# One tile for the high and low part of a weight, and twelve weight slots that begin at twelve places modulo 512 bytes

## The chip, the cores and the metric

The kernel runs on one core of one Trainium2 chip. The metric is the device time of one execution in microseconds. Before the change two runs took 986.48 and 988.05 us; their median is 987.26 us.

## The reference

The kernel computes an attention with a feature map and then two MLPs, all in float32:

```python
proj = einsum('bhsd,df->bhsf', x, w_phi)            # q and k: 4 batches, 8 heads, 576 rows, 64 wide; 128 features
proj = proj - max(abs(proj), axis=-1)
phi  = concatenate([exp(proj), exp(-proj)])
kv   = einsum('bhsf,bhsd->bhfd', phi(k), v); z = sum(phi(k), axis=2)
x    = einsum('bhsf,bhfd->bhsd', phi(q), kv) / (einsum('bhsf,bhf->bhs', phi(q), z) + 1e-06)
x    = x.transpose(0, 2, 1, 3).reshape(2304, 512)
h    = x @ w_in1;  x   = (h * cos(h)) @ w_out1                               # 512 -> 2048 -> 512
h    = x @ w_in2;  out = (max(h, 0) + alpha * min(h, 0)) @ w_out2            # 512 -> 2048 -> 512
```

The four weight matrices arrive as float64, seen by the kernel as pairs of 32-bit words.

## The kernel before

**The products.** A float32 product of the MLPs is made of three float32r matmuls: a number is split into a high part (float32r) and a low part (what is left, again float32r), and `mm3` (L160 to L166) sums high x high, high x low and low x high. Each matmul instruction loads its own stationary operand of 128 columns and then streams a moving operand of 512 or 256 columns past it. In the trace a matmul is named out<-moving,stationary.

**The order.** A step is one layer, one block of 128 of the 2048 hidden features (`ft`) and one group of 512 tokens (the last group has 256): 2 layers x 16 x 5 = 160 steps. `hidden` (L168) makes the hidden features of a step with 12 matmuls: stationary a 128 x 128 piece of the weight `wi` (high or low), moving the tokens `xh` or `xl`. `output` (L217) multiplies them into the output: in layer 0 the weight `wo` is stationary and the gated features `gh`, `gl` move; in layer 1 `gh`, `gl` are stationary and `wo` moves. `moe_step` runs the hidden part of one step, then the output part of an earlier step, and so on: 12 matmuls of `ph`, then 12 of `po` (6 where a layer-1 group has 256 tokens), through both layers.

**The weights.** `fetch_w` loads a 128 x 512 block of a weight as pairs of words. `w_instructions` (L95) lists the ten instructions that turn it into a high and a low part: ScalarE writes the high part (`to_hi`, L111, its copy at L116), GpSimd subtracts it (L134) and writes the low part (L135). These run some steps ahead of the use, at steps that a table `decode_at` holds. There are six slots for `wi` and six for `wo`, used in turn (slot = block number modulo 6). `w_tile` (L90) gives a slot's part a tile of 2048 bytes per partition, high and low apart, each with its own name: `wih0`, `wil0`, `wih1` and so on. Slots 0 and 1 lie in one pool, slots 2 to 5 in a second one, opened when the attention's tiles are closed.

**Where the tiles lie.** In the built program `xh`, `xl`, all 24 weight tiles, all `gh` and `gl` and the accumulators `acc` start 352 bytes past a multiple of 512, and the slices that a matmul takes of them are multiples of 512 bytes apart. So stationary and moving operand of every matmul of the MLPs start at the same place modulo 512. In what follows a tile's *place* is its start modulo 512, counted from the start of `xh`: here it is 0 for all.

**The attention.** It runs first, and its numerator (`num`, L574 to L586) is the one other float32r product: stationary `kvh` or `kvl` of 66 columns, moving `qp0h`, `qp0l` (256 columns) or `qp1h`, `qp1l` (320). A head's 66 columns are 264 bytes, a pair of heads 528, so these stationary operands start at many places, all multiples of 8 bytes and none 0 against their moving operand. The projections (`project`, L456) are plain float32 products. The last two blocks of `num` lie between the first `hidden` parts.

Of the kernel before, what the change touches and what calls it, by code (L numbers as in the profile page):

```python
# [12 lines left out]
F32R = mybir.dt.float32r  # L13
# [8 lines left out]
P = 128  # L22
# [6 lines left out]
def feature_map_attention_two_mlps(  # L29
# [15 lines left out]
    DM, DFF = w_in1.shape  # L45
# [6 lines left out]
    NFT = DFF // P  # L52
# [29 lines left out]
    w_t = {}  # L82
    w_pools, w_temps = [wpool], [wtmp]
    staged, decoding = [], []

    def split(hi, lo, src, lo_engine):
        nc.scalar.copy(hi, src)  # L87
        lo_engine.tensor_tensor(out=lo, in0=src, in1=hi.bitcast(F32), op=ALU.subtract)  # L88

    def w_tile(slot, nm):  # L90
        s = slot % WSLOTS
        pool = w_pools[0 if s < WSLOTS_A else 1]
        return pool.tile([P, DM], F32R, tag=f"{nm}{s}", name=f"{nm}{s}")

    def w_instructions(spare=True):  # L95

        layer, which, ft, st = staged.pop(0)
        w_temps.append(w_temps.pop(0))  # L100
        u = w_temps[0].tile([P, DM], F32, tag="wu", name="wu")
        t = w_temps[0].tile([P, DM], I32, tag="wt", name="wt")
        e = w_temps[0].tile([P, DM], I32, tag="we", name="we")
        w0, w1 = st[:, :, 0], st[:, :, 1]
        tf, ef = t.bitcast(F32), e.bitcast(F32)
        ts, stt = nc.vector.tensor_scalar, nc.vector.scalar_tensor_tensor
        tt = nc.gpsimd.tensor_tensor
        tv, copy = (nc.vector.tensor_tensor, nc.vector.tensor_copy) if spare else (tt, nc.scalar.copy)
        hl = []

        def to_hi():  # L111
            hl.extend(w_tile(layer * NFT + ft, f"w{'io'[which]}{x}") for x in "hl")
            w_t[layer, which, ft] = tuple(
                z.rearrange("p (k f) -> p k f", k=KD) if which == 0 else z for z in hl
            )
            copy(hl[0], tf)  # L116

        return [
            lambda: nc.scalar.activation(out=u, in_=w1.bitcast(F32), func=AF.Abs),
            lambda: ts(  # L120
                out=e, in0=w1, scalar1=0x07FFFFFF, scalar2=3, op0=ALU.bitwise_and,
                op1=ALU.logical_shift_left,
            ),
            lambda: stt(  # L124
                out=t, in0=w1, scalar=-0x40000000, in1=e, op0=ALU.bitwise_and, op1=ALU.bitwise_or
            ),
            lambda: stt(out=tf, in0=u, scalar=MIN_PATTERN, in1=tf, op0=ALU.is_ge, op1=ALU.mult),  # L127
            lambda: ts(out=e, in0=t, scalar1=-0x00800000, scalar2=None, op0=ALU.bitwise_and),
            to_hi,
            lambda: nc.scalar.activation(  # L130
                out=u, in_=w0.bitcast(U32), func=AF.Copy, scale=2.0 ** -52
            ),
            lambda: tt(out=u, in0=u, in1=ef, op=ALU.mult),  # L133
            lambda: tv(out=tf, in0=tf, in1=hl[0].bitcast(F32), op=ALU.subtract),  # L134
            lambda: tv(out=hl[1], in0=tf, in1=u, op=ALU.add),  # L135
        ]
# [140 lines left out]
    for i in range(2 * NFT):  # L277
        for which in range(2):
            w = (i // NFT, which, i % NFT)
# [17 lines left out]
    for latest in late[::-1][2 * WSLOTS_A:2 * W_EVEN]:  # L297
        need, free, w = todo.pop(0)
# [8 lines left out]
    for t in times:  # L307
        ready = [w for w in todo if w[1] <= t]
        if ready and (t > at + 1 or t >= latest[ready[0][2]]):
            need, _, w = ready[0]  # L310
# [490 lines left out]
```

## Time and profile before

| | us |
|---|---|
| median of two runs | 987.26 |
| the profiled execution | 987.01 |
| its span, first to last instruction | 985.2 |
| TensorE busy (matmul) | 978.3 |
| VectorE busy | 687.4 |
| GpSimd busy | 606.5 |
| ScalarE busy | 493.8 |

The profiled execution's own time is 1.8 us above its span. The profile models where a matmul ends: matmuls overlap in the records, so a matmul's duration (some 0.39 us) is longer than the distance from one start to the next, and it is that distance that adds up to the time.

### The profile page before, as it was taken

How to read it: one execution, taken by the hardware profiler on the slowest of the kernel's cores; microseconds unless marked ns; L12 is line 12 of the kernel's file. 1: busy time of each engine (PE TensorE's matmuls, PEld its weight loads, DVE VectorE, ACT ScalarE, POOL GpSimd, SP SyncE). 2: the span in 40 equal slices, each digit the busy share in tenths (PEclk: the TensorE clock that was granted, in tenths of full speed). 3: DMA queues.
4: the chain of work that ended last, by engine and by line, in shares of the span. 5: the costliest groups of instructions: out<-in, count | busy, mean ns of one | idle time of the engine just before them, and what ended most of it. 6: DMA issues, size and time to landing. Idle time of an engine off the chain costs nothing.

```text
span 985.2 us, 13990 instructions
## 1 busy us (share of the span) xinstructions
PE 978.3 (99%) x5141; PEld 839.2 (85%) x5141; DVE 687.4 (70%) x977; ACT 493.8 (50%) x967; POOL 606.5 (62%) x498
## 2 busy tenths in 40 slices
PE   9999999999999999999999999999999999999998
PEld 7999999888888888888888888888888888888886
DVE  6868686677987577747774788588748874885343
ACT  5888788867666467546755654132213221322110
POOL 3577777856666467535756789567636763676221
PEclk9999999999999999999999999999999999999999
DMA  7454543211111112101210112012101210110112
GB/s 165 113 140 124 142 121 109 70 48 56 52 66 45 42 43 65 44 22 43 65 44 22 44 43 65 22 43 65 43 22 44 65 43 22 43 65 1 43 55 95
DMA packets 64580, 60.63 MB, mean 62 GB/s; under 512 B 28928, under 2 KB 54656, under 8 KB 64512
## 3 DMA queue, kind: packets, MB, share of 16 engines
q1 hardware_dynamic: 64352, 59.68, 20.7%
q8 instruction: 40, 0.66, 0.3%
q14 instruction: 28, 0.23, 0.1%
q10 hardware_dynamic: 160, 0.07, 0.0%
HBM read 52.50 MB, written 4.79 MB: 58 GB/s over the span
## 4 chain that ended last, share of the span: by engine, by line
PE 95%; ACT 1%; DVE 1%; DMA 1%; POOL 1%; issue 0%; ACTq 0%; SPq 0%; DVEq 0%; POOLq 0%
PE po L165 39%; PE ph L165 38%; PE pj L456 6%; PE kv L497 5%; PE nm L581 5%; PE tp L537 1%; DMA dn<-acc 0%; DMA acc<-dr 0%; DMA w<-in_w_phi_dram 0%; DVE acc L616 0%; ACT acc L556 0%; DVE r L192 0%; DVE wt L127 0%; DMA dr<-dn 0%; ACT r L184 0%
## 5 line engine op out<-in xcount | busy, mean ns | idle before, releaser
L88 POOL TENSOR_TENSOR gl<-r,gh 128x512 fp32r<-128x512 f32 (+1 forms) x160 | 204.3, 1278 | 294.0 <-ACT gh L87 289.0
L87 ACT CAST gh<-r 128x512 fp32r<-128x512 f32 (+1 forms) x160 | 92.1, 576 | 381.4 <-DVE r L211 260.9
L165 PE MATMUL ph<-xl,wih 128*128 128x512 f32 (+1 forms) x640 | 236.0, 369 | 0.1
L165 PE MATMUL ph<-xh,wih 128*128 128x512 f32 (+1 forms) x640 | 235.7, 368 | 0.0
L165 PE MATMUL ph<-xh,wil 128*128 128x512 f32 (+1 forms) x640 | 235.6, 368 | 0.0
L245 DVE TENSOR_TENSOR acc<-po,acc 128x512 f32<-128x512 f32 (+1 forms) x134 | 86.1, 659 | 96.5 <-PE po L165 96.5
L165 PEld LDWEIGHTS ph<-xl,wih 128*128 128x128 f32 x640 | 120.7, 189 | 20.7 <-POOL xl L625 0.3
L165 PEld LDWEIGHTS ph<-xh,wih 128*128 128x128 f32 x640 | 120.7, 189 | 20.6
L165 PEld LDWEIGHTS ph<-xh,wil 128*128 128x128 f32 x640 | 120.6, 188 | 20.0
L165 PE MATMUL po<-gh,wol 128*128 128x512 f32 (+1 forms) x320 | 118.0, 369 | 0.2 <-POOL wol L135 0.2
L165 PE MATMUL po<-gl,woh 128*128 128x512 f32 (+1 forms) x320 | 118.0, 369 | 0.0
L165 PE MATMUL po<-gh,woh 128*128 128x512 f32 (+1 forms) x320 | 118.0, 369 | 0.0
L165 PE MATMUL po<-woh,gh 128*128 128x512 f32 x288 | 112.4, 390 | 0.0
L165 PE MATMUL po<-wol,gh 128*128 128x512 f32 x288 | 112.4, 390 | 0.0
L165 PE MATMUL po<-woh,gl 128*128 128x512 f32 x288 | 112.3, 390 | 0.0
L124 DVE SCALAR_TENSOR_TENSOR wt<-ws,we 128x512 int32<-128x512 int32 x64 | 98.4, 1537 | 2.4
L198 DVE TENSOR_SCALAR r<-ph,al 128x512 f32<-128x512 f32 (+1 forms) x80 | 55.3, 692 | 56.2 <-PE ph L165 36.7
L209 DVE TENSOR_TENSOR r<-ph,r 128x512 f32<-128x512 f32 (+1 forms) x80 | 50.5, 632 | 48.6 <-ACT r L196 48.4
L133 POOL TENSOR_TENSOR wu<-wu,we 128x512 f32<-128x512 f32 x64 | 82.9, 1295 | 1.3 <-ACT wu L130 1.3
L572 POOL TENSOR_TENSOR qp1l<-acc,qp1h 128x512 fp32r<-128x512 f32 (+1 forms) x64 | 59.1, 949 | 26.6 <-ACT qp1h L570 26.6
L497 PEld LDWEIGHTS kv<-vm,kp 128*128 128x128 f32 x512 | 72.6, 191 | 2.6 <-ACT qp1h L570 0.4
L497 PE MATMUL kv<-vm,kp 128*128 128x66 f32 x512 | 72.5, 255 | 0.1
(81 smaller groups left out, 1878.3 us busy)
## 6 DMA issues: line engine op xcount, KB each, us to landing
ws<-in_moe_w_in_dram SPq DMA_DIRECT2D x32, 512.0 KB, 3.7
ws<-in_moe_w_out_dram SPq DMA_DIRECT2D x32, 512.0 KB, 3.5
acc<-dr SPq DMA_DIRECT2D x32, 144.0 KB, 3.1
out_dram<-acc SPq DMA_DIRECT2D x18, 256.0 KB, 2.1
vm<-in_v_dram SPq DMA_DIRECT2D x16, 256.0 KB, 3.9
kin<-in_k_dram SPq DMA_DIRECT2D x28, 128.0 KB, 3.0
qin<-in_q_dram SPq DMA_DIRECT2D x28, 128.0 KB, 2.8
acc<-acc SPq DMA_DIRECT2D x16, 144.0 KB, 2.4
```

Source lines behind the costliest of these rows:

```text
L87: nc.scalar.copy(hi, src)
L88: lo_engine.tensor_tensor(out=lo, in0=src, in1=hi.bitcast(F32), op=ALU.subtract)
L124: lambda: stt(out=t, in0=w1, scalar=-0x40000000, in1=e, op0=ALU.bitwise_and, op1=ALU.bitwise_or),
L133: lambda: tt(out=u, in0=u, in1=ef, op=ALU.mult),
L165: nc.tensor.matmul(ps, lhsT=l, rhs=r, start=(first and m == 0), stop=(last and m == n - 1))
L198: nc.vector.tensor_scalar(out=r, in0=ph, scalar1=0.0, scalar2=al[:, ft:ft + 1], op0=ALU.min, op1=ALU.mult)
L209: nc.vector.tensor_tensor(out=r, in0=ph, in1=r, op=ALU.mult)
L245: nc.vector.tensor_tensor(out=a, in0=po, in1=a, op=ALU.add)
L456: nc.tensor.matmul(pj[:, a].rearrange("p j f -> p (j f)"), lhsT=x[:, a * P:(a + 1) * P], rhs=w2.rearrange("p j f -> p (j f)"), start=True, ...
L497: nc.tensor.matmul(ps[:, :, y, :] if pr is None else ps[:, pr, y, :], lhsT=e[:, s, 2 * a + y, :], rhs=vt[:, y] if pr is None else vm[:, pr ...
L572: nc.gpsimd.tensor_tensor(out=dl, in0=et, in1=dh.bitcast(F32), op=ALU.subtract)
L581: nc.tensor.matmul(nm, lhsT=l[:, s, pr, y * VW:(y + 1) * VW], rhs=r[:, s, y, :], start=(s == 0 and m == 0), stop=(s == 1 and m == 2),)
```

## The change

`w_tile` is replaced by `w_pair`, which allocates one tile per slot for both parts, with unused bytes ahead (`lead`) and behind (`rest`). The lead is chosen so that the high part starts at the place that the table gives; the low part starts 2048 bytes later, so at the same place modulo 512. The rest makes the tile's size a multiple of 32, and `moved` keeps the sum of all unused bytes so far.

```diff
+    place = {
+        "wi": (4, 8, 16, 448, 480, 272),
+        "wo": (12, 24, 20, 40, 80, 208),
+    }
+    moved = [0]
+    spare_of = {}
...
-    def w_tile(slot, nm):
+    def w_pair(slot, nm):
         s = slot % WSLOTS
         pool = w_pools[0 if s < WSLOTS_A else 1]
-        return pool.tile([P, DM], F32R, tag=f"{nm}{s}", name=f"{nm}{s}")
+        if (nm, s) not in spare_of:
+            lead = (place[nm][s] - moved[0]) % 512
+            rest = -lead % 32
+            moved[0] += lead + rest
+            spare_of[nm, s] = lead // 4, rest // 4
+        lead, rest = spare_of[nm, s]
+        t = pool.tile([P, lead + 2 * DM + rest], F32R, tag=f"{nm}{s}", name=f"{nm}{s}")
+        return [t[:, lead + x * DM:lead + (x + 1) * DM] for x in range(2)]
...
         def to_hi():
-            hl.extend(w_tile(layer * NFT + ft, f"w{'io'[which]}{x}") for x in "hl")
+            hl.extend(w_pair(layer * NFT + ft, "w" + "io"[which]))
```

The twelve places in bytes are 4, 8, 16, 448, 480, 272 for the slots of `wi` and 12, 24, 20, 40, 80, 208 for those of `wo`. Two of them (448, 480) are multiples of 32, four (16, 272, 80, 208) leave 16, three (8, 24, 40) are multiples of 8 only, and three (4, 12, 20) of 4 only. The tiles behind the slots of the first pool move up by 1568 bytes, 49 times 32, together: `acc` and the attention's tiles of the same side among them, `kvh`, `kvl` and `qp0h` to `qp1l` by the same amount. `xh`, `xl`, `gh` and `gl` stay where they were.

In the built program every engine has the same instructions as before in the same order. The semaphores that they wait for are the same too but for one place: at the first decode in the second pool, GpSimd's wait for a matmul of the attention, which stood ahead of the subtraction at L134, stands two instructions earlier, ahead of the multiplication at L133 (where a wait for an earlier matmul stood).

## Rows read from the trace of the kernel before

**Rows 1.** The page's busy time of each engine, with its share of the span.
```profile
PE 978.3 (99%) x5141; PEld 839.2 (85%) x5141; DVE 687.4 (70%) x977; ACT 493.8 (50%) x967; POOL 606.5 (62%) x498
```
**Rows 2.** The page's chain that ended last, by engine and by line.
```profile
PE 95%; ACT 1%; DVE 1%; DMA 1%; POOL 1%; issue 0%; ACTq 0%; SPq 0%; DVEq 0%; POOLq 0%
PE po L165 39%; PE ph L165 38%; PE pj L456 6%; PE kv L497 5%; PE nm L581 5%; PE tp L537 1%; DMA dn<-acc 0%; DMA acc<-dr 0%; DMA w<-in_w_phi_dram 0%; DVE acc L616 0%; ACT acc L556 0%; DVE r L192 0%; DVE wt L127 0%; DMA dr<-dn 0%; ACT r L184 0%
```
**Rows 3.** Busy us by stretch: PE, PEld, DVE, ACT, POOL; clock, DMA share, GB/s.
```profile
0.00:188.00 188.00, 185.42 (x1369) 172.13 (x1369) 139.98 (x238) 152.41 (x354) 129.59 (x130) 1.00 0.48 123
210.00:985.00 775.00, 770.91 (x3665) 648.53 (x3663) 534.32 (x721) 325.24 (x585) 462.93 (x358) 1.00 0.14 46
```
**Rows 4.** All that TensorE waited for: engine and line, us in total, times, longest.
```profile
PE tp L433 <- DVE half_pi L435: 1.6, 1, 1.6
PE pj L456 <- DMA w<-in_w_phi_dram: 0.5, 1, 0.5
PE tp L537 <- ACT qp0h L570: 0.4, 1, 0.4
PE po L165 <- POOL wol L135: 0.2, 1, 0.2
```
**Rows 5.** TensorE's groups by shape: count, busy us, mean ns, idle us.
```profile
L165 PE MATMUL ph<-xh,wih 128*128 128x512 f32 x512 | 199.6, 390 | 0.0
L165 PE MATMUL po<-woh,gh 128*128 128x512 f32 x288 | 112.4, 390 | 0.0
L165 PE MATMUL po<-gh,woh 128*128 128x512 f32 x256 | 99.9, 390 | 0.0
L165 PE MATMUL ph<-xl,wih 128*128 128x256 f32 x128 | 36.4, 284 | 0.1
L165 PE MATMUL po<-gh,wol 128*128 128x256 f32 x64 | 18.1, 284 | 0.0
```
**Rows 6.** TensorE's matmuls in order of time: start us, duration us; 512 columns.
```profile
284.94 0.39 PE L165 MATMUL ph<-xl,wih 128*128 128x512 f32 x1
...
299.90 0.39 PE L165 MATMUL ph<-xl,wih 128*128 128x512 f32 x1
```
**Rows 7.** The same view, from 512 columns to 256 and back to 512.
```profile
277.03 0.28 PE L165 MATMUL po<-gh,woh 128*128 128x256 f32 x1
277.14 0.28 PE L165 MATMUL po<-gl,woh 128*128 128x256 f32 x1
277.26 0.28 PE L165 MATMUL po<-gh,wol 128*128 128x256 f32 x1
...
278.46 0.40 PE L165 MATMUL ph<-xh,wih 128*128 128x512 f32 x1
278.70 0.40 PE L165 MATMUL ph<-xl,wih 128*128 128x512 f32 x1
...
279.62 0.39 PE L165 MATMUL ph<-xh,wil 128*128 128x512 f32 x1
```
**Rows 8.** The same view, plain float32 projections of 256 columns in the attention.
```profile
100.34 1.03 PE L456 MATMUL pj<-w,kin 128*128 128x256 f32 x4
101.20 1.03 PE L456 MATMUL pj<-w,qin 128*128 128x256 f32 x4
```
**Rows 9.** The same view, float32r numerators with operands at different places.
```profile
39.45 0.31 PE L581 MATMUL nm<-qp1h,kvl 128*66 128x320 f32 x1
...
40.32 0.31 PE L581 MATMUL nm<-qp1h,kvl 128*66 128x320 f32 x1
...
192.35 0.28 PE L581 MATMUL nm<-qp0h,kvh 128*66 128x256 f32 x1
...
192.71 0.40 PE L165 MATMUL ph<-xh,wih 128*128 128x512 f32 x1
```
**Rows 10.** Instructions on the weight tiles: min, median, max ns; first and last start.
```profile
L116 ACT CAST wih<-wt x32: 612/616/666, 46.1 to 869.5; 128x512 fp32r<-128x512 f32 x32
L134 POOL TENSOR_TENSOR wt<-wt,wih x32: 1280/1300/1487, 53.6 to 872.2; 128x512 f32<-128x512 f32 x32
L135 POOL TENSOR_TENSOR wil<-wt,wu x32: 1292/1297/1671, 54.9 to 873.6; 128x512 fp32r<-128x512 f32 x32
L134 POOLq EVENT_SEMAPHORE  x1: 17/17/17, 212.8 to 212.8; - x1
```
**Rows 11.** GpSimd's largest group: busy us, mean ns, idle before it, releaser.
```profile
L88 POOL TENSOR_TENSOR gl<-r,gh 128x512 fp32r<-128x512 f32 (+1 forms) x160 | 204.3, 1278 | 294.0 <-ACT gh L87 289.0 <-issue 4.8
```

## The prediction

> **What bounds the kernel now.** I read the busy times first: the matmuls fill 978.3 of 985.2 us [rows 1]. The chain that ended last says the same: 95% of it is TensorE, and L165, the one line of all MLP matmuls, holds 39% (`po`) and 38% (`ph`) [rows 2]. By stretches, TensorE is busy for 770.91 of the 775 us from 210 us on, while VectorE has 534, GpSimd 463 and ScalarE 325 [rows 3]. All that TensorE ever waited for is 2.7 us, of which 0.2 us was a weight that GpSimd had not yet written [rows 4]. So no engine, DMA or wait limits the MLPs; what counts is the distance from one matmul's start to the next.
>
> How many there are comes from the groups by shape [rows 5]. Of 512 columns: three groups of 512 (`ph`), three of 288 (`po`, weight moving) and three of 256 (`po`, weight stationary), 3168 in all. Of 256 columns: three of 128 and three of 64, 576 in all. Together 3744.
>
> How far apart they start comes from the view in order of time. From 284.94 to 299.90 us there are 67 matmuls of 512 columns, 66 distances: 14.96 / 66 = 0.2267 us [rows 6]. For 256 columns, from 277.14 to 278.46 us are 11 distances: 1.32 / 11 = 0.120 us [rows 7]. 3168 x 0.2267 + 576 x 0.120 = 718.1 + 69.1 = 787.2 us, four fifths of the time.
>
> The clock was granted in full in both stretches (1.00, the 2.4 GHz level) [rows 3], where 512 columns need 213.3 ns and 256 need 106.7. So each matmul takes 13.3 ns longer than its columns, at both widths. That is the number that matters, for stationary and moving operand lie at the same place modulo 512 in every one of these. I call it the surplus. One nanosecond of it is 3744 x 0.001 = 3.74 us of the kernel, or 0.38%; 2% of the time, about what a measurement of this kernel can tell from no change, is 19.7 us or 5.3 ns a matmul.
>
> Two rows say that the surplus isn't a constant. A plain float32 projection of 256 columns starts every (101.20 - 100.34) / 4 = 0.215 us [rows 8]: at half the rate, 512 column times, it has a surplus of only 2 ns, with the same 128-column weight load. And with all operands at place 0, the first matmul of 256 columns after a run of 512 starts the next after 0.11 us (113 ns in the record, which the view rounds), the others 0.12; the first of 512 columns after a run of 256 takes 0.24, and the first five take 279.62 - 278.46 = 1.16 us, 0.232 each, before the distance is 0.2267 again [rows 7]. Nothing differs there but how the weight load stands against the stream in time. A weight load that reads at the same time as the moving operand, and holds it up more or less, would look like this; then a place would matter as a time does.
>
> **The change part by part.**
>
> *The matmuls.* All 3744 get another distance between their operands: in 1920 `ph` and 960 `po` of layer 0 the stationary operand moves, in 864 `po` of layer 1 the moving one. No row shows a 128-column weight at another place. The nearest are the attention's numerators, float32r too, whose 66-column weights start 8, 16, 24 or 0 modulo 32 from the moving operand, and never at the same place modulo 512. From 39.45 to 40.32 us are six distances at 320 columns: 0.145 us each, surplus 145 - 133.3 = 11.7 ns; from 192.35 to 192.71 three at 256 columns, the last with a 128-column weight load of `ph` beside it: 0.120, surplus 13.3 [rows 9]. Over all 116 such distances of the attention that have numerators on both sides, the records give a mean surplus of 12.3 ns (40 of 256 columns: 11.2; 76 of 320: 12.9), singly from 6 to some 20, and starts that are 8 or 24 modulo 32 are no worse than 0 or 16. Against 13.3 that is -0.4 to -2.1 ns, and I take the mean over all, -1.0 ns: 3744 x -1.0 = -3.7 us. The bounds, from rows far off: below, the projections' surplus of 2 ns, 3744 x -11.3 = -42 us; above, a moving operand that is read at half rate. The projections show what half rate costs: 0.215 us for 256 columns, so 0.43 for 512. Places 4, 12 and 20 are no multiples of 8, and no row has such an operand; two of them are `wo` slots (0 and 2), which stream in layer 1 in 5 of 16 blocks: 5 x 18 x 3 = 270 matmuls x 0.2 us = +54 us. I take neither: the attention's rows are the nearest.
>
> *Changes of place.* Before, only the width changes from step to step. Now each `ph` block of a step and each `po` block has another place, 320 blocks. If each change upset the stream as the change from 256 to 512 columns does, 1.16 - 5 x 0.2267 = 0.027 us, that is +8.5 us; if as the change from 512 to 256, about -7 ns each, -2.2 us. I take 0, between them, because the attention's mean already comes from runs of six and fewer in which places change.
>
> *The decode.* ScalarE writes the high part (616 ns), GpSimd reads it (1300) and writes the low one (1297), 64 times each [rows 10]. I cost another address at 0. At double time GpSimd would have 64 x 2.6 = 166 us more; its `gl` group alone shows 294 us of idle time, 289 of it waiting for ScalarE [rows 11], and decodes run steps ahead, which is why TensorE waited 0.2 us for them [rows 4]. If that cover went, the cost would show as waits of `po` and `ph` for L135. Below nothing it can't matter, as TensorE doesn't wait for it.
>
> *One tile for two parts.* A slot is free for the new high part only when the old low part has been read too. The last reader of the low part comes one matmul after that of the high part, 0.23 us, and the decode begins after both by its table: 0. The one wait that moves is GpSimd's at L134, 17 ns long at 212.8 us [rows 10]: its matmul had ended, so ahead of L133 it ends at most one instruction later. Behind it stands that decode and the next `gl` (L88), for which `po` would wait; 0.
>
> *The sum.* 987.01 (own time of the profiled execution; 0.25 under the median) - 3.7 = 983.3 us, own range 978 (all at 11.2 ns, 3744 x -2.1 = -7.9) to 996 (8.5 for changes of place).
>
> The Trainium skill, "TensorE: Matmul & The Clock Gate", section "Step-by-step: what each phase is for", speaks against any effect: it says that TensorE has two independent SBUF read ports, so that loading the next weights takes no read bandwidth from the running matmul. By that rule places do nothing and the time is 987.0. The trace does not bear it out clearly: the 0.11 and 0.24 us beside 0.12 and 0.2267 at one place [rows 7] need something that the two share.
>
> **The rivals.**
>
> *Places do nothing (N).* The surplus belongs to float32r, as it is nearly the same at 256, 320 and 512 columns and with 66 or 128 weight columns. Time: 987.0. For it: the attention's mean differs by only 1 ns. Against it: the single distances there go from 6 ns to 20.
>
> *The surplus mostly goes (F).* Equal places make load and stream want the same piece of SBUF each time, and shifted ones don't. The 113 ns start shows a surplus of 6.3 ns with a 128-column load: 3744 x -7.0 = -26 us, 961; with the projections' surplus 945. For it: the lock at exactly 13.3 ns over hundreds of matmuls at place 0, while shifted places scatter. Against: none of the attention's groups stays at 6 ns.
>
> *The stream is upset at shifted places and stays so (S).* The five matmuls behind a change of width take 0.232 us, 5.3 ns more than in the steady run. Should the shifted operands hold the stream in that state, with a new place every 12 matmuls, all 3744 pay: +19.8 us, 1007. At the 0.24 us of its first start, +13 ns, it is 1036, and half-rate reads of the operands that are no multiple of 8 bytes give 1041. It decides from 5.3 ns a matmul on. For it: twelve matmuls are hardly more than the five or six that settling takes. Against: the attention's runs, which change places as often, show 0.145 and 0.120, not more.
>
> **How the numbers follow.** The forecast has 0.30, N 0.23; both lie within 2%: 0.53. F has 0.25, nearly all of it under 967.5: faster 0.25. S has 0.22: slower. The likeliest is 983.3 us. For the range I leave out one tenth at each end: F from 955 up (surplus 4.8 ns) and S up to 1022 (9.3 ns more) stay in.
>
> **What would show it.** Right: in the view in order of time the `ph` and `po` starts stand 0.224 to 0.228 apart at 512 columns and 0.117 to 0.121 at 256 whatever the slot, with the waits of TensorE still under 4 us, and 3744 matmuls as before. N: 0.2267 in every slot. F: 0.216 to 0.220 in most slots. S: 0.232 or more. By slot the distances tell which places do what: slots 448 and 480 of `wi` against 4, 8 and 16, and layer 0 against layer 1 for `wo`. I am wrong in kind if the distances stay and the time moves: then TensorE would show new waits for L135, and the decode's durations at L116, L134, L135 (plus 13 lines) would have grown.

## The result and the profile after

The changed kernel takes 999.94 us (median of 999.84 and 1000.05) against 987.26: a ratio of 1.0128, 95% interval 1.0085 to 1.0172. It is slower by 12.7 us. The forecast was 983.3 us, 3.7 us less than the execution it started from.

The page's busy times, and its chain that ended last, for the changed kernel (they answer to [rows 1] and [rows 2]; line numbers are 13 higher):

```profile
span 998.2 us, 13989 instructions
...
PE 991.5 (99%) x5141; PEld 837.8 (84%) x5141; DVE 683.8 (68%) x977; ACT 493.8 (49%) x967; POOL 601.5 (60%) x498
...
PE 98%; ACT 1%; DMA 0%; DVE 0%; issue 0%; ACTq 0%
PE po L178 40%; PE ph L178 40%; PE pj L469 6%; PE kv L510 5%; PE nm L594 5%; PE tp L550 2%; DMA w<-in_w_phi_dram 0%; ACT acc L569 0%; ACT qp1h L583 0%; ACT qp0h L583 0%; ACT acc L607 0%; ACT kp L498 0%; DVE acc L489 0%; DVE mx L481 0%; DVE acc L258 0%
```

TensorE is busy for 13.2 us more, the span is 13.0 us longer, the other engines are where they were or a little lower. By stretches (columns as in [rows 3]):

```profile
0.00:188.00 188.00, 185.24 (x1375) 171.84 (x1376) 141.19 (x238) 153.24 (x356) 130.63 (x131) 1.00 0.48 124
210.00:985.00 775.00, 774.98 (x3624) 640.73 (x3624) 525.32 (x713) 323.97 (x584) 457.20 (x357) 1.00 0.14 44
```

The attention is as it was. From 210 to 985 us the clock is granted in full as before, and TensorE starts 3624 matmuls where it had started 3665 [rows 3]: 41 fewer in the same time. It doesn't wait for anything new (columns as in [rows 4]):

```profile
PE tp L446 <- DVE half_pi L448: 1.6, 1, 1.6
PE tp L550 <- ACT qp0h L583: 0.4, 1, 0.4
PE pj L469 <- DMA w<-in_w_phi_dram: 0.3, 1, 0.3
PE pj L469 <- DVE acc L489: 0.3, 1, 0.3
```

The groups by shape show where the time is (columns as in [rows 5]; high and low weight now have one name, so two groups of before make one):

```profile
L178 PE MATMUL ph<-xh,wi 128*128 128x512 f32 x1024 | 340.8, 394 | 0.0
L178 PE MATMUL po<-wo,gh 128*128 128x512 f32 x576 | 180.7, 395 | 0.0
L178 PE MATMUL po<-gh,wo 128*128 128x512 f32 x512 | 170.5, 394 | 0.0
...
L178 PE MATMUL ph<-xl,wi 128*128 128x256 f32 x128 | 35.9, 280 | 0.0
```

In the profile a matmul's duration is its distance to the next start plus a nearly constant part (390 for 227 before). It went from 390 to 394 and 395 ns at 512 columns and from 284 to 280 at 256 [rows 5]: the wide matmuls became slower, the narrow ones faster.

TensorE's matmuls in order of time, the first one of each of four blocks of 12 in layer 0 and of the block behind. By the program's order of steps the slots are `wi2` (place 16), `wo3` (40), `wi3` (448), `wo2` (20):

```profile
257.79 0.40 PE L178 MATMUL ph<-xh,wi 128*128 128x512 f32 x1
...
260.60 0.39 PE L178 MATMUL po<-gh,wo 128*128 128x512 f32 x1
...
263.39 0.39 PE L178 MATMUL ph<-xh,wi 128*128 128x512 f32 x1
...
266.14 0.40 PE L178 MATMUL po<-gh,wo 128*128 128x512 f32 x1
...
268.94 0.40 PE L178 MATMUL ph<-xh,wi 128*128 128x512 f32 x1
```

12 distances take 2.81, 2.79, 2.75 and 2.80 us: 0.234, 0.2325, 0.229 and 0.233 each, against 0.2267 in [rows 6]. And a block of 256 columns, slot `wo0` (place 12), the same view:

```profile
238.32 0.27 PE L178 MATMUL po<-gh,wo 128*128 128x256 f32 x1
...
239.72 0.39 PE L178 MATMUL ph<-xh,wi 128*128 128x512 f32 x1
```

1.40 / 12 = 0.117, against 0.120 in [rows 7].

All starts of the trace, sorted by the slot they use, give these mean distances in ns (real waits over 260 ns left out):

| 512 columns | place: mean distance |
|---|---|
| before, every slot | 0: 227.0 to 227.5 |
| after, `ph`, `wi` stationary | 4: 232.2, 8: 231.0, 16: 233.0, 448: 229.6, 480: 233.0, 272: 231.5 |
| after, `po` of layer 0, `wo` stationary | 12: 231.1, 24: 230.8, 20: 232.9, 40: 233.0, 80: 231.8, 208: 232.1 |
| after, `po` of layer 1, `wo` moving | 12: 229.3, 24: 233.8, 20: 237.3, 40: 233.5, 80: 230.8, 208: 233.9 |

Over all slots 512 columns went from 227.1 to 232.1 ns (4.96 more) and 256 columns from 119.5 to 117.8. 3168 x 4.96 - 576 x 1.8 = 15.7 - 1.0 = +14.7 us. The span grew by 13.0; of the rest, 1.1 us is that matmul distances over 260 ns, the real waits, add up to 1.2 us after and 2.3 before, and the first `ph` starts 0.9 us earlier.

The distances don't settle at 227 within a block. From the first few matmuls on they repeat a pattern of the slot, such as 232, 226, 229 at place 448 or 229, 229, 234, 230, 231 at place 8. Of 256 blocks of 512 columns only 6 have a mean under 227.5 ns (five of them at place 272), and the first six distances of the blocks have the same mean as the last six (232.1 and 232.0). So the distance goes with the place, and what remained to be found was which property of it, and how much a change of place adds. Whether the one tile costs anything by itself had to be shown too.

### The profile page after: what moved, and what is told of

It reads as the page before. It is cut to its first block, busy times and chain, and to the rows that moved or that the text cites. A ratio compares the mean times of both kernels' runs of the same rounds, so it can differ in the third digit from the quotient of the medians.

```text
span 998.2 us, 13989 instructions
## 1 busy us (share of the span) xinstructions
PE 991.5 (99%) x5141; PEld 837.8 (84%) x5141; DVE 683.8 (68%) x977; ACT 493.8 (49%) x967; POOL 601.5 (60%) x498
## 4 chain that ended last, share of the span: by engine, by line
PE 98%; ACT 1%; DMA 0%; DVE 0%; issue 0%; ACTq 0%
PE po L178 40%; PE ph L178 40%; PE pj L469 6%; PE kv L510 5%; PE nm L594 5%; PE tp L550 2%; DMA w<-in_w_phi_dram 0%; ACT acc L569 0%; ACT qp1h L583 0%; ACT qp0h L583 0%; ACT acc L607 0%; ACT kp L498 0%; DVE acc L489 0%; DVE mx L481 0%; DVE acc L258 0%
## 5 line engine op out<-in xcount | busy, mean ns | idle before, releaser
L178 PE MATMUL ph<-xh,wi 128*128 128x512 f32 (+1 forms) x1280 | 391.1, 371 | 0.0
L178 PEld LDWEIGHTS ph<-xh,wi 128*128 128x128 f32 x1280 | 233.9, 188 | 45.3
L178 PE MATMUL ph<-xl,wi 128*128 128x512 f32 (+1 forms) x640 | 237.2, 371 | 0.0
L178 PE MATMUL po<-gh,wo 128*128 128x512 f32 (+1 forms) x640 | 195.8, 371 | 0.0
L178 PE MATMUL po<-wo,gh 128*128 128x512 f32 x576 | 180.7, 395 | 0.0
L178 PEld LDWEIGHTS ph<-xl,wi 128*128 128x128 f32 x640 | 120.3, 188 | 23.3 <-POOL xl L638 0.2
L178 PEld LDWEIGHTS po<-gh,wo 128*128 128x128 f32 x640 | 116.7, 188 | 22.7 <-POOL wo L148 0.2
L178 PEld LDWEIGHTS po<-wo,gh 128*128 128x128 f32 x576 | 107.3, 188 | 23.9
L178 PE MATMUL po<-gl,wo 128*128 128x512 f32 (+1 forms) x320 | 118.8, 371 | 0.0
L178 PE MATMUL po<-wo,gl 128*128 128x512 f32 x288 | 113.8, 395 | 0.0
L178 PEld LDWEIGHTS po<-gl,wo 128*128 128x128 f32 x320 | 60.1, 188 | 11.3
```

The costliest lines, as they stand in the source:

```text
L178: nc.tensor.matmul(ps, lhsT=l, rhs=r, start=(first and m == 0), stop=(last and m == n - 1))
```

## The experiments

Each diff is against the changed kernel, if nothing else is said; lines left out of a diff stand as `...`, and behind the first diff the two lines that are replaced (`-`) are not printed again. Runs without an interval are single runs. On the same chips the kernel before took 986.4 to 987.3 us, and 13 runs of it on one of them lie between 986.1 and 988.5, so a difference of 6 us or more is far outside what runs differ by.

**One tile, all places 0.**

```diff
-        "wi": (4, 8, 16, 448, 480, 272),
-        "wo": (12, 24, 20, 40, 80, 208),
+        "wi": (0, 0, 0, 0, 0, 0),
+        "wo": (0, 0, 0, 0, 0, 0),
```

> High and low part stay in one tile per slot, all twelve places are 0. Theory P (the place itself sets the distance between matmuls): 987 us as before, 0.227 us at 512 columns, 0.120 at 256 in every slot. Rival M (the one tile, through its waits, costs the time): 1000 us, with new waits of TensorE.

986.88 us; ratio to the kernel before 1.0003, interval 0.9993 to 1.0013. The groups by shape are back at the durations of [rows 5]:

```profile
L178 PE MATMUL ph<-xh,wi 128*128 128x512 f32 x1024 | 335.9, 389 | 0.0
...
L178 PE MATMUL po<-wo,gh 128*128 128x512 f32 x576 | 177.7, 390 | 0.0
```

M falls: the one tile costs nothing. All of the 12.7 us are the places.

**One place, 16, for all slots.**

```diff
...
+        "wi": (16, 16, 16, 16, 16, 16),
+        "wo": (16, 16, 16, 16, 16, 16),
```

> One place, 16, for all twelve slots, so that in layer 0 weight and moving operand stand the same way in every matmul. Theory P: 0.230 to 0.235 us at 512 columns in every block of both layers, 1000 to 1008 us. Rival S (each change of place upsets the stream, which then settles at the old distance): layer 0 back at 0.227 us, layer 1, where ph and po still differ, at 0.23; some 993 us.

995.18 us, between the two. Three blocks of layer 0 in order of time (first matmul of each):

```profile
283.71 0.40 PE L178 MATMUL ph<-xh,wi 128*128 128x512 f32 x1
...
286.51 0.39 PE L178 MATMUL po<-gh,wo 128*128 128x512 f32 x1
...
289.31 0.39 PE L178 MATMUL ph<-xh,wi 128*128 128x512 f32 x1
```

2.80 / 12 = 0.233 us, block after block, though in layer 0 nothing changes its place here. S, as it is put for this run, can't explain that. But P, as it was written, fails too: of the 192 blocks of 512 columns with a stationary weight, 101 run at 227 ns from their fifth matmul on and 91 at 233 or 234. At one place the stream has two states that keep themselves. In layer 0 one block of 512 columns never differs in its state from the one right before it; behind the attention's last matmuls the state changes only across a block of 256 columns or a real wait. So what came before picks the state.

**Multiples of 32.**

```diff
...
+        "wi": (32, 64, 128, 192, 320, 384),
+        "wo": (64, 96, 192, 256, 384, 416),
```

> All places are multiples of 32: 32, 64, 128, 192, 320, 384 for wi and 64, 96, 192, 256, 384, 416 for wo. If only the remainder modulo 32 counts (rival R): 0.227 us in every slot, 987 us. If the place modulo 512 counts (P): slots differ, 0.226 to 0.234 us, as places 448 and 480 did in the changed kernel (0.2296 and 0.233); 995 to 1003 us.

1000.7 us, in P's range: R falls. One block, slot `wi5` at 384, and the first matmul behind it:

```profile
283.13 0.39 PE L178 MATMUL ph<-xh,wi 128*128 128x512 f32 x1
...
285.91 0.39 PE L178 MATMUL po<-gh,wo 128*128 128x512 f32 x1
```

2.78 / 12 = 0.232 us. By slot the means are 229.0 to 233.6 ns. Two things stand out: place 192 repeats 231, 226, 229 ns, the pattern of place 448 = 192 + 256 in the changed kernel; and at place 256 the blocks begin at 226 to 236 ns but end at 227, as at place 0. That suggested that addresses count modulo 256. (In the changed kernel, 272 = 16 + 256 shows the same two states, 227 and 233, as place 16 above; its mean, 231.5 against 233.0 at place 16, is another mixture of them.)

**`xh`, `xl` and `wi` shifted by 8 bytes together, `wo`, `gh`, `gl` at 0.**

```diff
+    xhl = xpool.tile([P, 2 + 2 * KD * NTOK + 6], F32R, name="xhl")
+    xh, xl = (
+        xhl[:, 2 + x * KD * NTOK:2 + (x + 1) * KD * NTOK].rearrange("p (k t) -> p k t", k=KD)
+        for x in range(2)
+    )
...
+        "wi": (8, 8, 8, 8, 8, 8),
+        "wo": (0, 0, 0, 0, 0, 0),
...
+    moved = [32]
```

> xh, xl and all six wi slots shifted by 8 bytes together, wo, gh and gl at 0: every operand pair stands at equal places again, but those of ph begin 8 bytes off a multiple of 32. If the difference of the two places counts: ph and po at 0.227 us, 987 us. If the address of an operand itself counts: ph at 0.230 to 0.234 us, po at 0.227, some 994 us.

994.54 us. Ten matmuls of a `ph` block (x10), and the first `po` behind them:

```profile
283.73 2.47 PE L181 MATMUL ph<-xhl,wi 128*128 128x512 f32 x10
286.04 0.39 PE L181 MATMUL po<-gh,wo 128*128 128x512 f32 x1
```

2.31 / 10 = 0.231 us. `ph` repeats 230, 231, 232 ns over its whole block, although weight and moving operand stand at equal places; `po` has long first matmuls (about 242 and 232) and is then at 227, mean 228.6. So the difference of the two places isn't all: the addresses themselves count.

**The same with 32 bytes.**

```diff
+    xhl = xpool.tile([P, 8 + 2 * KD * NTOK], F32R, name="xhl")
...
+        "wi": (32, 32, 32, 32, 32, 32),
+        "wo": (0, 0, 0, 0, 0, 0),
...
```

> xh, xl and the six wi slots shifted together by 32 bytes, wo, gh and gl at 0. If an operand pair at equal places is fast wherever both start at a multiple of 32: ph 0.227 us, po 0.227, 987 us. If only their start against a multiple of some larger size counts: ph 0.230 to 0.233 us as with 8 bytes, 994 us.

993.35 us: near the time of the second answer (994), but not for its reason. A `po` block in order of time (x2 stands for two matmuls), and the first `ph` behind it:

```profile
285.77 0.39 PE L181 MATMUL po<-gh,wo 128*128 128x512 f32 x1
...
286.70 0.39 PE L181 MATMUL po<-gl,wo 128*128 128x512 f32 x1
...
287.38 0.39 PE L181 MATMUL po<-gl,wo 128*128 128x512 f32 x1
...
288.06 0.39 PE L181 MATMUL po<-gl,wo 128*128 128x512 f32 x1
...
288.52 2.23 PE L181 MATMUL ph<-xhl,wi 128*128 128x512 f32 x9
```

The first four distances take 0.93 us, 0.2325 each, the next two threes 0.68, 0.2267 each. `ph` does the same: seven distances from 224 to 236 ns, then 227. Equal places at 32 do settle at the fast distance, as those at 0 do, but each change between pairs at 0 and pairs at 32 costs: a block's mean is 229.3 instead of 227.1. So S had a part of the truth; a change of place can cost by itself, some 2.2 x 12 = 26 ns a block here.

**All places 256; and `wi` at 256 with `wo` at 0.**

The first of the two:

```diff
...
+        "wi": (256, 256, 256, 256, 256, 256),
+        "wo": (256, 256, 256, 256, 256, 256),
```

> All twelve places are 256, so that weight and moving operand stand 256 bytes apart in every matmul of both layers and no change of place happens at all. Theory P2 (place 256 has the same settled distance as place 0; the long first matmuls of its blocks in the run with multiples of 32 came from the change of place): 0.227 us throughout, 987 to 990 us. Rival (every place but 0 is slower by itself): 0.229 us or more, 994 us.

> All wi slots at place 256, all wo slots at 0: both places settle at 0.227 us when they stand alone, but ph and po now alternate between them. If a change of place costs by itself (part of theory S): some seven matmuls of 0.226 to 0.236 us at the head of each block, then 0.227; 7 x 4 ns x 300 = 8 us, 995 us. If only the place counts: 0.227 us throughout, 987 us.

986.45 and 986.29 us, both as before. In the second one (its `wo` zeros) a `po` block, the `ph` block behind and the next `po`:

```profile
284.63 0.39 PE L178 MATMUL po<-gh,wo 128*128 128x512 f32 x1
...
287.35 0.39 PE L178 MATMUL ph<-xh,wi 128*128 128x512 f32 x1
...
290.07 0.39 PE L178 MATMUL po<-gh,wo 128*128 128x512 f32 x1
```

2.72 / 12 = 0.2267 us in both, with no long matmul at a block's head. P2 holds, and the cost that a change between 0 and 256 could have had is not there: these times don't tell the two places apart. With the pairs 192 and 448, 16 and 272, this fits addresses that count modulo 256 at most.

**Twelve more places.**

```diff
...
+        "wi": (28, 48, 112, 144, 200, 232),
+        "wo": (56, 72, 176, 184, 240, 248),
```

> Twelve more places: 28, 48, 112, 144, 200, 232 for wi and 56, 72, 176, 184, 240, 248 for wo. Theory P: every slot between 0.229 and 0.235 us at 512 columns, none under 0.2267, 998 to 1006 us. Rival: some place is better than 0, which would show as a slot under 0.2267 us.

1001.14 us. Stationary weights: 228.2 (place 240) to 233.2 ns; moving ones 232.2 to 234.6. Place 240 falls just under the expected band, and none comes under place 0. With the runs above, some thirty places are known, and of the slots moved by themselves only those at 0 and 256 settle at 227 ns in nearly every block of every run. Place 16 is not alone in having two states: here `wi` at 28 settles at 227 in 12 of its 24 blocks, stationary `wo` at 240 in 3 of 8, and in the changed kernel `wi` at 272 in 6 of 20. So a place doesn't fix one distance; it fixes which patterns are possible.

**Whose reads they are: operands that stay in one spot.** Four kernels that leave the tiles of the kernel before as they are and read less of one operand, so that the products are others. The diffs are against the kernel before.

```diff
+                l = l[:, 0:1].to_broadcast([P, l.shape[-1]])
                 nc.tensor.matmul(ps, lhsT=l, rhs=r, start=(first and m == 0), stop=(last and m == n - 1))
```

> The kernel before, but every stationary operand of the MLP products is its first column, read 128 times (so the products are not the reference's). Theory C (the 13.3 ns come from the weight load reading SBUF beside the moving stream): the distance changes, to 0.216 us at 512 columns if the load no longer holds the stream up, some 945 us. Rival N (the surplus belongs to float32r): 0.2267 us, 987 us.

995.05 us, neither. The distances in order of time:

```profile
286.39 0.40 PE L166 MATMUL po<-gh,wol 128*128 128x512 f32 x1
286.62 0.39 PE L166 MATMUL po<-gh,woh 128*128 128x512 f32 x1
286.85 0.40 PE L166 MATMUL po<-gl,woh 128*128 128x512 f32 x1
287.08 0.40 PE L166 MATMUL po<-gh,wol 128*128 128x512 f32 x1
```

0.69 us for three; the records have 226, 234, 233 over and over, in every slot and from the first matmul on, and 113 ns at 256 columns where 120 stood. So neither answer came. The stream and its addresses are those of the kernel before, and only what the load reads is other: that does change the stream's pace. It didn't free the stream.

```diff
+                r = r[:, 0:1].to_broadcast([P, r.shape[-1]])
                 nc.tensor.matmul(ps, lhsT=l, rhs=r, start=(first and m == 0), stop=(last and m == n - 1))
```

> The kernel before, but every moving operand of the MLP products is its first column, read 512 or 256 times (so the products are not the reference's). Theory C: the distance changes from 0.2267 us, to about 0.216 if the stream now reads one address and is out of the load's way. Rival N: 0.2267 us, 987 us.

951.78 us. A `ph` and a `po` block, from the first matmul to the first behind them:

```profile
283.74 0.38 PE L166 MATMUL ph<-xh,wih 128*128 128x512 f32 x1
...
288.93 0.38 PE L166 MATMUL ph<-xh,wih 128*128 128x512 f32 x1
```

5.19 / 24 = 0.216 us, 2.9 ns over the 213.3 that the prediction counts for the columns, with the whole weight loads beside it. So the surplus is not float32r's own: the reason that N gave falls. With the first four columns (16 bytes) read over and over,

> The kernel before, but the moving operand of the MLP products is its first four columns (16 bytes), read 128 or 64 times (so the products are not the reference's). If the load and the stream only meet where their addresses run through the same range: near 0.216 us at 512 columns, as with one column, 950 us. If the stream needs a new read of SBUF for every few columns whatever their address: 0.227 to 0.233 us, 987 to 1005 us.

it is the same, 951.88 us and 216 ns. With the first 64 columns (256 bytes):

> The kernel before, but the moving operand of the MLP products is its first 64 columns (256 bytes), read 8 or 4 times (so the products are not the reference's). If only the address modulo 256 counts, as the equal times at places 0 and 256 suggest, this stream looks like the whole one: 0.2267 us at 512 columns, 0.120 at 256, the same 987 us. If more of the address counts: another distance, between 0.216 and 0.234 us.

986.37 us, and the same two blocks as in the kernel before:

```profile
284.70 0.39 PE L167 MATMUL po<-gh,woh 128*128 128x512 f32 x1
...
287.42 0.39 PE L167 MATMUL ph<-xh,wih 128*128 128x512 f32 x1
...
290.14 0.39 PE L167 MATMUL po<-gh,woh 128*128 128x512 f32 x1
```

0.2267 us again. A stream that runs through the same 256 bytes eight times takes the same time as one of 2048 bytes; the two streams that stay within 16 bytes lose nearly all of the surplus. Lengths between were not tried. The products are others here too, and the time is that of the kernel before, so it isn't the changed values that make the other two faster.

## Why the prediction was wrong

**What bounds the kernel: right.** The time moved by the distances alone, at a clock granted in full, with no new wait. That the weight load and the stream bear on each other is shown twice: in `ph` only the weight moved, and the stream went from 227.0 to between 229.6 and 233.0 ns; with a load of one column it took 231. What the stream itself reads counts too (216 ns within 16 bytes). No run takes the load away, so how much of the 13.3 ns at place 0 comes from the meeting of the two, and how much from the stream's reads alone, stays open. One rule was set against any effect. The Trainium skill, "TensorE: Matmul & The Clock Gate", section "Step-by-step: what each phase is for", says that loading the next weights takes no SBUF read bandwidth from the running matmul. It would have left 987 us; here the measurement differs, 227 against 232 ns with nothing but addresses changed.

**The step that failed: "I take the mean over all, -1.0 ns".** It carried a mean of the attention's numerators to matmuls of 512 columns. At 256 columns it was right in sign: -1.0 in the sum, -2.1 from the numerators of that width, -1.8 measured. At 512 columns it had the wrong sign: +5.0 ns instead of -1.0, a surplus of 232.1 - 213.3 = 18.8 ns where the sum had 12.3. No row had a float32r matmul of 512 columns at another place, and the numerators of 256 and 320 columns, with a weight of 66, were no price for it. The equal surplus of 13.3 ns at both widths hid this, as it is that of place 0 alone: not what any place would give, but at 512 columns a good state that shifting loses.

It is tempting to find a warning in the rows: the numerators' surplus was 11.2 ns at 256 columns and 12.9 at 320, and a line through the two gives 18 at 512. But that line was drawn afterwards, and it doesn't hold. In the changed kernel the same distances have a mean surplus of 11.3 and 11.8 ns, and the line through them gives some 13 at 512. What the rows did say is that no width beyond 320 had been seen at another place; why 512 columns lose where 256 gain was not found.

The measured time lies inside the stated 955 to 1022 us, but by the share that S had in it. The sum's own range, 978 to 996, was missed, since it took 11.2 ns and the changes of place for its bounds.

**The changes of place: taken at 0.** In the changed kernel they can't be seen apart from the places, since hardly a block settles at 227. Alone, they cost nothing between 0 and 256 and some 26 ns a block between pairs at 0 and at 32 (measured in one run), close to the 27 ns that [rows 7] gave for a change of width.

**The decode, the one tile, the wait: right at 0.** The instructions on the weight tiles take as long as in [rows 10]:

```profile
L129 ACT CAST wi<-wt x32: 613/616/662, 45.4 to 879.4; 128x512 fp32r<-128x512 f32 x32
L147 POOL TENSOR_TENSOR wt<-wt,wi x32: 1087/1296/1492, 52.9 to 882.0; 128x512 f32<-128x512 f32 x32
L148 POOL TENSOR_TENSOR wi<-wt,wu x32: 1288/1302/1813, 54.1 to 883.2; 128x512 fp32r<-128x512 f32 x32
```

**The rivals.** N fell with the changed kernel, and its reason with the one-column stream. F is true of that stream but of no place. S named the size, 0.232 us, and the direction, but put it on 256 columns as well (1007 us). Its reason, that a stream which gets a new place every 12 matmuls never settles, is not the main one: with place 16 everywhere blocks of layer 0 followed each other at one place and one width and still ran at 233. That such a state keeps itself, as S said, is borne out there. The half-rate read of operands that are multiples of 4 alone didn't come: `wo` at 12 moves at 229.3 ns, at 20 at 237.3.

## What to carry to other kernels

Where TensorE streams float32r operands of 512 columns back to back, let stationary and moving operand of all of them begin at one and the same place modulo 256 bytes, on a multiple of 32 (0 and 32, and 0 against 256, are what was tried): here that was worth 5 ns of 232 on every such matmul, and a padding that looks harmless can lose it. At 256 columns the shifted places were 1.8 ns the better ones, so measure at the width that you have. When a cost is carried from one shape to another, ask for a row of that shape first; a mean over narrower shapes is no price for a wider one, and a line through two of them is none either. And before improving a figure that is the same everywhere, find a row where it is otherwise, to learn whether the present state is the usual one or a lucky one.

## What was not expected of the hardware

- Distances repeat patterns of a few matmuls that go with the two addresses, such as 232, 226, 229 ns at places 192 and 448; at places 16, 28 and 272 two states are seen, 227 and some 233 ns, and with place 16 in all slots matmuls of 512 columns stay in the one that they fell into.
- The addresses count, and not only their difference: equal places 8 give 231 ns. The attention's numerators show it too: where both their operands moved together by 32 or 96 bytes beyond a multiple of 256 (the changed kernel, place 16, multiples of 32, the twelve more places), their mean surplus at 320 columns is 11.5 to 11.8 ns; in all other runs, where they stayed or moved by a multiple of 256, it is 12.4 to 13.2.
- A stream that stays within 16 bytes runs at 216 ns for 512 columns, beside full weight loads: what the stream reads makes 3.6% of the kernel's time (951.8 against 987 us) even at the best place.
- A weight load of one column read 128 times doesn't free the stream (231 ns).
- Which part of the memory the two reads meet in was not found, nor why equal places 8 give 231 ns and equal places 0 and 32 settle at 227. No version clearly faster than the kernel before came out of the places tried: of the slots at 512 columns none has a mean under 226.9 ns, and the most that a slot saves at 256 columns (`wo` at place 192: 114.8 ns against 119.5) would be worth 576 x 4.7 = 2.7 us if all had it; that was not tried alone.
